# Two small constant tables of an attention kernel made from a memset and one index selection in place of two iotas

## The chip, the cores and the metric

The kernel runs on one core of one Trainium2 chip. The metric is the device time of one execution in microseconds. The kernel before took 751.49 us, the median of three runs that lie between 751.37 and 751.6. One execution was recorded by the hardware profiler; it took 750.43 us, and its first and last instruction are 748.9 us apart.

The engines are called as in the profile: PE (TensorE), PEld (its weight loads), DVE (VectorE), ACT (ScalarE), POOL (GpSimd) and SP (SyncE, which here only issues transfers). A name with a "q" (POOLq, SPq) is that engine's instruction queue. POOL's more complex instructions come in libraries of code that are loaded while the program runs; an instruction whose library is not known to be there has a load put ahead of it when the program is built, and the program can ask for a load by hand (`load_library`).

## The reference

Two blocks over 2048 tokens of width 640, with 32 heads of 20 columns, their outputs side by side:

```
# A: attention with a softmax
q, k, v = split_heads(A_x @ A_wqkv)
p = softmax(q @ k^T * 20**-0.5)
a = concat_heads(p @ v) @ A_wo

# B: linear attention
phi(t) = where(t > 0, t + 1, exp(t)) + 1e-6
num = phi(q) @ (phi(k)^T @ v);  den = phi(q) . sum(phi(k)) + 1e-6
b = concat_heads(num / den) @ B_wo

out = concat([a, b], axis=-1)          # (1, 2048, 1280), bf16
```

## The kernel before, in words

**The work.** Almost all of it lies in the class `_Fast`. Four heads make a group, each with 32 rows of the 128 partitions: 20 rows of data, one row (row 20 of the 32) that carries a constant, the rest zero. Scores are computed in blocks of 512 queries by 128 keys per head. A part of the exponentials is done by ACT (L1833, from PSUM to `f_PT`), another part by DVE and POOL with integer arithmetic (DVE L1731 writes `f_Sr`, POOL L1904 adds to it as 64-bit integers). PE then multiplies either with V. Projections, block B and the output projection are fitted between these steps.

**What sets the order.** A planner with estimated costs (`plan`, `run`) decides when the program is built in which order each engine gets its instructions, and `_Sched` adds the semaphore waits that the data needs. On the chip each engine takes its queue in that fixed order. The plan starts its clock at 8500 ns for all engines, behind the part that the change touches, and knows nothing of library loads.

**The start of the kernel.** `start_loads` (L1019) issues the first four tiles of x (tokens 0 to 511, 128 a tile, into `f_st`) from SP, the two weight strips for the first group of Q and K (`wst0`, part of the arena `f_ar`) from ACT's queue, then from SP the next 512 tokens, the weights of V, ten transposing loads for the last 1024 tokens (L1046), and the weights of K and Q (L1050, L1051).

`consts` (L1057), written out by hand, then does this:

- POOL makes an index table with an iota (L1060); DVE compares it with zero and so has the 128 x 128 identity `f_id` (L1065).
- POOL makes a second, two-column table of the partition numbers with another iota (L1067). That waits for DVE, because it overwrites the first. Then POOL is told to load library 1 by hand (L1069), the library of the 64-bit addition.
- DVE takes the partition number modulo 32 (L1070), and from it the masks: `kb` (1 or 16256 on row 20 of each 32, L1072 and L1074, and a bf16 copy, L1077) and `km` (1 or the factor `cq` on rows 0 to 19, L1078 and L1080).
- PE, meanwhile, runs 16 matmuls on zeros (`heat`, in the trace L156 with `f_zt`), waits for the identity, transposes the four tiles of x (20 transposes, L1093), and runs 8 more matmuls on zeros.
- DVE (L1100) and ACT (L1103) copy the transposed tiles to `f_xT`, two each.
- The two weight strips are spread into groups of 32 columns: DVE writes 20 columns of each (L1107), POOL the other 12 (L1110). Both parts of `wqp` are inputs of the first Q projection.
- POOL sets the column of ones in V and Vp (L1113, L1114).

Then POOL fills three Q buffers and seven groups of K with the constant rows out of the bf16 mask (`wprep`, L1124 and L1129) and clears two slices of the output weights (L1136).

The first steps of the plan are the Q projection of group 0 (PE, then DVE L1256 into `f_Qr`, with `km` and `kb` as factor and addend, and L1219 into `f_sq`), the K projection (L1256 into `f_KT`, L1235 into `f_ar`), tiles of V (L1303), and the first scores. The copies in `f_sq` and `f_ar` hold columns of other groups, which SP moves to their place with small transfers (L1195).

`_general` is a second, slower version of block A, taken only if a flag computed at the end asks for it. It has iotas of its own, and the change leaves it as it is.

Of the kernel before, what the change touches and what calls it, by code (L numbers as in the profile page):

```python
# [12 lines left out]
ALU = mybir.AluOpType  # L13
AX = mybir.AxisListType
# [3 lines left out]
D_HEAD = 20  # L18
# [751 lines left out]
class _Fast:  # L770
# [285 lines left out]

    def consts(self):  # L1057
        sch, ps = self.sch, self.ps
        it = self.it
        sch.op("pool", lambda e: e.iota(it[:, 0:128], [[1, 128]], base=0, channel_multiplier=-1),  # L1060
               writes=("it",))
        sch.op("dve", lambda e: e.memset(self.zt[:], 0.0), writes=("zt",))
        sch.op("dve", lambda e: e.memset(self.warm[:], 0.0), writes=("warm",))
        sch.op("act", lambda e: e.activation(self.warm[:], self.warm[:], AF.Exp), writes=("warm",))
        sch.op("dve", lambda e: e.tensor_scalar(self.ident[:], it[:, 0:128], 0.0, None, op0=ALU.is_equal),  # L1065
               reads=("it",), writes=("ident",))
        sch.op("pool", lambda e: e.iota(it[:, 0:2], [[0, 2]], base=0, channel_multiplier=1),  # L1067
               reads=("ident",), writes=("it",))
        self.nc.gpsimd.load_library(library_config.all_libraries[1])  # L1069
        sch.op("dve", lambda e: e.tensor_scalar(it[:, 2:4], it[:, 0:2], 31, None, op0=ALU.bitwise_and),  # L1070
               reads=("it",), writes=("it2",))
        sch.op("dve", lambda e: e.tensor_scalar(self.kb[:, 0:1], it[:, 2:3], float(D_HEAD), None, op0=ALU.is_equal),  # L1072
               reads=("it2",), writes=("kb0",))
        sch.op("dve", lambda e: e.tensor_scalar(self.kb[:, 1:2], it[:, 2:3], float(D_HEAD), 16256.0,  # L1074
                                                op0=ALU.is_equal, op1=ALU.mult),
               reads=("it2",), writes=("kb1",))
        sch.op("dve", lambda e: e.tensor_copy(self.kb16[:], self.kb[:]), reads=("kb0", "kb1"), writes=("kb16",))  # L1077
        sch.op("dve", lambda e: e.tensor_scalar(self.km[:, 1:2], it[:, 2:3], float(D_HEAD), None, op0=ALU.is_lt),  # L1078
               reads=("it2",), writes=("km1",))
        sch.op("dve", lambda e: e.tensor_scalar(self.km[:, 0:1], it[:, 2:3], float(D_HEAD), self.cq,  # L1080
                                                op0=ALU.is_lt, op1=ALU.mult),
               reads=("it2",), writes=("km0",))
        zt = self.zt

        def heat(k):
            for _ in range(k):
                sch.mm(ps[:, 6, 0:256], zt[:, 0:128], zt[:], start=True, stop=True, reads=("zt",),
                       writes=(("ps", 6),))
        heat(16)
        for t in range(4):  # L1090
            pb = ps[:, t, :].bitcast(BF16)
            for c in range(N_DC):
                sch.op("pe", lambda e, c=c, t=t, pb=pb: e.transpose(  # L1093
                    pb[:, 128 * c:128 * (c + 1)], self.stage[:, t, 128 * c:128 * (c + 1)], self.ident[:]),
                    reads=(("xn", t), "ident"), writes=(("ps", t),), inc=(c == N_DC - 1))
            heat(8 if t == 3 else 0)
            dst = self.xT[:, :, 128 * t:128 * (t + 1)]
            src = pb[:, 0:D_MODEL].rearrange("p (c m) -> p c m", c=N_DC)
            if t % 2 == 0:
                sch.op("dve", lambda e, dst=dst, src=src: e.tensor_copy(dst, src),  # L1100
                       reads=(("ps", t),), writes=(("xt", t),))
            else:
                sch.op("act", lambda e, dst=dst, src=src: e.copy(dst, src),  # L1103
                       reads=(("ps", t),), writes=(("xt", t),))
        for k, (wp, nm) in enumerate(((self.wqp, "wqp"), (self.wkp, "wkp"))):
            dst = wp[:, 0].rearrange("p c (i r) -> p c i r", r=32)
            sch.op("dve", lambda e, dst=dst, k=k: e.tensor_copy(  # L1107
                dst[:, :, :, 0:D_HEAD], self.wst0[:, k, :, 0:80].rearrange("p c (i d) -> p c i d", d=D_HEAD)),
                reads=(("wst0", k),), writes=((nm, 0),))
            sch.op("pool", lambda e, dst=dst, k=k: e.tensor_copy(  # L1110
                dst[:, :, :, D_HEAD:32], self.wst0[:, k, :, 80:128].rearrange("p c (i d) -> p c i d", d=12)),
                reads=(("wst0", k),), writes=((nm, 1),))
        sch.op("pool", lambda e: e.memset(self.V[:, :, :, 0:1], 1.0), writes=("Vones",))  # L1113
        sch.op("pool", lambda e: e.memset(self.Vp[:, :, :, 0:1], self.WP), writes=("Vones",))  # L1114
        sch.op("dve", lambda e: e.memset(ps[:, self.PVB, :], 0.0), writes=(("ps", self.PVB),))
        sch.op("dve", lambda e: e.memset(self.ones[:], 1.0), writes=("ones",))
        for e in self.free:
            self.free[e] = 8500.0
# [1206 lines left out]
```

## Time and profile before

| what | value |
|---|---|
| median of three runs | 751.49 us (751.37 to 751.6) |
| the profiled execution | 750.43 us |
| its span, first to last instruction | 748.9 us |
| PE busy | 721.3 us (96%) |
| ACT busy | 709.1 us (95%) |
| DVE busy | 619.9 us (83%) |
| POOL busy | 323.0 us (43%) |
| mean granted clock of PE | 0.989 |
| first POOL instruction of `consts` | starts at 9.19 us |
| first scores | start at 22.01 us |

A page of the profile gives the busy time of each engine, then the span in 40 equal slices (a digit is the busy share in tenths, and in the row PEclk the granted clock in tenths), and the chain that ended last, followed back from the last instruction to what released it at each step. The chain can also be printed in order of time, each piece with its start, its length and what it was. The timeline gives, for a group of equal instructions, its start, its length, engine, line, operation, output and input, shapes and count, and in brackets how long the engine had been idle before and which instruction ended that. In the table by stretches, each engine has its busy time and its instructions, followed by the granted clock, the busy share of the DMA engines and GB/s. "issue" is time in which the engine waited for nothing that the profile shows; a library load is not an instruction of the profile.

### The profile page before, as it was taken

The numbers are of one execution on the slowest core, as the hardware profiler recorded it, in microseconds if no ns is written. First come the engines' busy times: TensorE is split into PE (matmuls) and PEld (weight loads), VectorE is DVE, ScalarE is ACT, GpSimd is POOL, SyncE is SP. The second block draws the span as 40 slices with busy tenths as digits, with TensorE's granted clock in tenths as the row PEclk, the third lists the DMA queues.
The fourth block names the chain that finished last, engine by engine and source line by source line (L and its number), as shares of the span: only waits on it lengthen the run. The fifth ranks groups of instructions, "written<-read, shape, count | busy, mean of one in ns | idle before, by whom it ended". The sixth has DMA issues, their size and how long they took to land.

```text
span 748.9 us, 25688 instructions
## 1 busy us (share of the span) xinstructions
PE 721.3 (96%) x11193; PEld 254.7 (34%) x11193; DVE 619.9 (83%) x1179; ACT 709.1 (95%) x802; POOL 323.0 (43%) x313
## 2 busy tenths in 40 slices
PE   5999999999999999999999999999999999999995
PEld 3533333333222333333333333233233333332333
DVE  1888976787888888888889878899898989998973
ACT  1599999999999999999999999999999999999993
POOL 1924444054455444425433236642155554442550
PEclk7999999999999999999999999999999999999999
DMA  7411010101610100201101003011021100000001
GB/s 200 144 25 40 4 38 11 34 12 38 140 37 11 40 19 9 42 7 30 27 7 37 20 8 93 14 34 34 21 48 36 36 29 9 14 28 15 7 19 59
DMA packets 42611, 27.67 MB, mean 37 GB/s; under 512 B 26891, under 2 KB 41931, under 8 KB 42491
## 3 DMA queue, kind: packets, MB, share of 16 engines
q1 hardware_dynamic: 41178, 25.62, 13.2%
q8 instruction: 90, 1.47, 0.8%
q10 hardware_dynamic: 1312, 0.33, 0.2%
q14 instruction: 31, 0.25, 0.1%
HBM read 8.40 MB, written 5.24 MB: 18 GB/s over the span
## 4 chain that ended last, share of the span: by engine, by line
PE 44%; ACT 41%; DVE 6%; POOL 3%; issue 3%; DMA 1%; SPq 0%; DVEq 0%; POOLq 0%; ACTq 0%
PE ps L156 43%; ACT f_PT L1833 39%; POOL f_Sr L1904 3%; DVE f_Sr L1731 2%; ACT ps L1386 2%; DVE f_T L1924 1%; PE ps L1004 1%; DVE f_T L1931 1%; SPq L1195 0%; DVE f_ar L1388 0%; DMA f_ar<-in_B_x_dram 0%; DVE f_ar L1235 0%; DMA f_KT<-f_ar 0%; DVE f_ar L1384 0%; DVE f_sq L1219 0%
## 5 line engine op out<-in xcount | busy, mean ns | idle before, releaser
L1833 ACT ACTIVATE f_PT<-ps 128x1024 bf16<-128x1024 f32 x742 | 693.6, 1101 | 17.2 <-PE ps L156 16.0
L1904 POOL INT64_ADD f_Sr<-f_Sr x282 | 299.7, 1076 | 386.2 <-PE ps L156 293.0
L1731 DVE TENSOR_SCALAR f_Sr<-ps 128x512 int16<-128x512 f32 x564 | 381.0, 683 | 59.6 <-PE ps L156 53.7
L156 PE MATMUL ps<-f_Qr,f_KT 32*128 32x512 bf16 x2048 | 292.5, 384 | 5.6 <-ACT f_PT L1833 3.8
L156 PEld LDWEIGHTS ps<-f_Qr,f_KT 32*128 32x128 bf16 x2048 | 73.4, 91 | 247.3 <-ACT f_PT L1833 220.0
L156 PE MATMUL ps<-f_ar 128*32 128x320 bf16 (+4 forms) x3024 | 150.2, 295 | 1.1 <-DVE f_Sr L1731 0.4
L156 PE MATMUL ps<-f_PT,f_V 128*21 128x512 bf16 x1484 | 142.1, 382 | 0.0
L156 PE MATMUL ps<-f_Sr,f_V 128*21 128x512 bf16 x1128 | 103.6, 383 | 2.1 <-POOL f_Sr L1904 0.9
L156 PEld LDWEIGHTS ps<-f_ar 128*32 128x32 bf16 x3024 | 61.3, 95 | 63.9 <-issue 35.2
L156 PE MATMUL ps<-f_Sr,f_Vp 128*21 128x512 bf16 x564 | 54.1, 383 | 1.0 <-POOL f_Sr L1904 0.8
L156 PEld LDWEIGHTS ps<-f_PT,f_V 128*21 128x21 bf16 x1484 | 36.1, 90 | 42.8 <-issue 37.6
L156 PEld LDWEIGHTS ps<-f_Sr,f_V 128*21 128x21 bf16 x1128 | 26.5, 90 | 39.6 <-issue 19.1
L156 PE MATMUL ps<-f_ar,f_xT 128*32 128x160 bf16 x1280 | 37.1, 237 | 0.6 <-DVE f_ar L1235 0.4
L989 DVE CAST f_st<-ps 128x320 bf16<-128x320 f32 x60 | 28.6, 480 | 8.8 <-PE ps L156 8.6
L1388 DVE SCALAR_TENSOR_TENSOR f_ar<-ps,f_ar 128x320 bf16<-128x320 f32 (+1 forms) x52 | 28.9, 556 | 5.6 <-ACT ps L1386 5.0
L156 PE MATMUL ps<-f_xT,f_ar 128*32 128x512 bf16 x400 | 31.9, 396 | 0.3 <-DVE f_xT L1169 0.2
L156 PE MATMUL ps<-f_wo,f_OTd 128*32 128x320 bf16 (+1 forms) x608 | 31.6, 301 | 0.0
L1386 ACT ACTIVATE ps<-ps 128x320 f32<-128x320 f32 (+1 forms) x52 | 31.0, 596 | 0.0
L1384 DVE TENSOR_SCALAR f_ar<-ps 128x320 f32<-128x320 f32 (+1 forms) x52 | 28.8, 553 | 2.6 <-PE ps L156 2.6
L1924 DVE TENSOR_TENSOR f_T<-f_T,f_Rt 128x512 bf16<-128x512 f32 x32 | 29.4, 919 | 0.1
L156 PEld LDWEIGHTS ps<-f_ar,f_xT 128*32 128x32 bf16 x1280 | 23.6, 97 | 16.5 <-issue 9.6
L1303 DVE CAST f_V<-ps 128x160 bf16<-128x160 f32 x64 | 19.6, 316 | 10.4 <-PE ps L156 10.4
(72 smaller groups left out, 310.5 us busy)
## 6 DMA issues: line engine op xcount, KB each, us to landing
out_dram<-f_st SPq DMA_DIRECT2D x32, 160.0 KB
f_ar<-in_B_wqkv_dram SPq DMA_DIRECT2D x3, 800.0 KB
f_OTd<-f_OTn SPq DMA_DIRECT2D x105, 20.0 KB
f_Qr<-f_sq SPq DMA_DIRECT2D x88, 20.0 KB
f_KT<-f_ar SPq DMA_DIRECT2D x22, 80.0 KB
f_ar<-in_A_wqkv_dram SPq DMA_DIRECT2D x2, 800.0 KB
f_wq<-in_A_wqkv_dram SPq DMA_DIRECT2D x1, 800.0 KB
f_wo<-in_A_wo_dram SPq DMA_DIRECT2D x1, 800.0 KB
```

The costliest lines, as they stand in the source:

```text
L156: lambda e: e.matmul(out, lhsT, rhs, start=start, stop=stop, tile_position=tp, skip_group_check=sgc),
L989: (lambda e: e.tensor_copy(sl, ps[:, b, 0:320])), (("ps", b),), (("stage", s, h),),
L1004: self.sch.op("pe", lambda e, m=m: e.transpose(m["out"], m["in"], m["id"]), reads=m["reads"], writes=m["writes"], inc=m.get("inc", k == le ...
L1303: self.push("dve", lambda e: e.tensor_copy(dst, src), (("ps", b), "Vones"), (("V", t, r),), _c_dve(w), prio=1, after=None if isd else last)
L1384: self.push("dve", lambda e: e.tensor_scalar(r1, src, 0.0, 1e-6, op0=ALU.max, op1=ALU.add), (("ps", b),), (rk,), _c_dve(n), prio=1, ok=ok, ...
L1386: "act", lambda e: e.activation(src, src, AF.Exp), (), (("ps", b),), _c_act(n), prio=0,
L1388: "dve", lambda e: e.scalar_tensor_tensor(dst, src, 1.0, r1, op0=ALU.min, op1=ALU.add),
L1731: post = lambda: self.push("dve", lambda e: e.tensor_scalar(self.Sr[:, s, i, :], self.ps[:, b, :], 0.0, 32639.0 - self.PH[-1], op0=ALU.max ...
L1833: return _Op("act", lambda e: e.activation(self.PT[:, s0:s0 + n, :], ps[:, b0:b0 + n, :], AF.Exp, scale=math.log(2.0) / 128.0, bias=self.l ...
L1904: self.q["pool"].append(_Op("pool", lambda e: e.int64_add(v, v, inc), res, res, self.C64, self.C64 + 150, 0, self.seq, after))
L1924: "dve", lambda e: e.tensor_tensor(T2v, Tv, R.unsqueeze(2).broadcast_to([128, 16, 32]), op=ALU.mult),
L1931: self.push("dve", lambda e: e.transpose(self.T[:], ps[:, b, :]), (("ps", b),), ("T",), 630, prio=-1, after=freed, ok=lambda: n == 0 or (" ...
```

## The change

The change is in `consts` alone.

- Library 1 is asked for first, ahead of any POOL instruction of `consts`.
- The identity is made on POOL: a memset of `f_id` to 1, then one index selection (`affine_select`) that keeps the ones on the diagonal and writes zero elsewhere. Library 1 holds this selection as well. The comparison on DVE goes.
- The masks come from the identity. Row p has its one in column p, so among the columns 20, 52, 84 and 116 (column 20 of each block of 32) a row has a one exactly if p modulo 32 is 20, and among the columns 0 to 19 of each block exactly if p modulo 32 is below 20. Two maximum reductions on DVE (4 and 80 elements) give `kb[:, 0]` and `km[:, 1]`, and two products give the other two columns.
- Both iotas, the index table and the operation modulo 32 go.

```diff
     def consts(self):
         sch, ps = self.sch, self.ps
-        it = self.it
-        sch.op("pool", lambda e: e.iota(it[:, 0:128], [[1, 128]], base=0, channel_multiplier=-1),
-               writes=("it",))
+        self.nc.gpsimd.load_library(library_config.all_libraries[1])
+        idn = self.ident
+        sch.op("pool", lambda e: e.memset(idn[:], 1.0), writes=("ident",))
+        sch.op("pool", lambda e: e.affine_select(idn[:], idn[:], [[-1, 128]], ALU.is_equal, 0.0, base=0,
+                                                 channel_multiplier=1), writes=("ident",))
         sch.op("dve", lambda e: e.memset(self.zt[:], 0.0), writes=("zt",))
         sch.op("dve", lambda e: e.memset(self.warm[:], 0.0), writes=("warm",))
         sch.op("act", lambda e: e.activation(self.warm[:], self.warm[:], AF.Exp), writes=("warm",))
-        sch.op("dve", lambda e: e.tensor_scalar(self.ident[:], it[:, 0:128], 0.0, None, op0=ALU.is_equal),
-               reads=("it",), writes=("ident",))
-        sch.op("pool", lambda e: e.iota(it[:, 0:2], [[0, 2]], base=0, channel_multiplier=1),
-               reads=("ident",), writes=("it",))
-        self.nc.gpsimd.load_library(library_config.all_libraries[1])
-        sch.op("dve", lambda e: e.tensor_scalar(it[:, 2:4], it[:, 0:2], 31, None, op0=ALU.bitwise_and),
-               reads=("it",), writes=("it2",))
-        sch.op("dve", lambda e: e.tensor_scalar(self.kb[:, 0:1], it[:, 2:3], float(D_HEAD), None, op0=ALU.is_equal),
-               reads=("it2",), writes=("kb0",))
-        sch.op("dve", lambda e: e.tensor_scalar(self.kb[:, 1:2], it[:, 2:3], float(D_HEAD), 16256.0,
-                                                op0=ALU.is_equal, op1=ALU.mult),
-               reads=("it2",), writes=("kb1",))
+        iv = idn[:].rearrange("p (b c) -> p b c", c=32)
+        sch.op("dve", lambda e: e.tensor_reduce(self.kb[:, 0:1], iv[:, :, D_HEAD], axis=AX.X, op=ALU.max),
+               reads=("ident",), writes=("kb0",))
+        sch.op("dve", lambda e: e.tensor_reduce(self.km[:, 1:2], iv[:, :, 0:D_HEAD], axis=AX.XY, op=ALU.max),
+               reads=("ident",), writes=("km1",))
+        sch.op("dve", lambda e: e.tensor_scalar(self.kb[:, 1:2], self.kb[:, 0:1], 16256.0, None, op0=ALU.mult),
+               reads=("kb0",), writes=("kb1",))
         sch.op("dve", lambda e: e.tensor_copy(self.kb16[:], self.kb[:]), reads=("kb0", "kb1"), writes=("kb16",))
-        sch.op("dve", lambda e: e.tensor_scalar(self.km[:, 1:2], it[:, 2:3], float(D_HEAD), None, op0=ALU.is_lt),
-               reads=("it2",), writes=("km1",))
-        sch.op("dve", lambda e: e.tensor_scalar(self.km[:, 0:1], it[:, 2:3], float(D_HEAD), self.cq,
-                                                op0=ALU.is_lt, op1=ALU.mult),
-               reads=("it2",), writes=("km0",))
+        sch.op("dve", lambda e: e.tensor_scalar(self.km[:, 0:1], self.km[:, 1:2], self.cq, None, op0=ALU.mult),
+               reads=("km1",), writes=("km0",))
         zt = self.zt
```

## The prediction

> **What bounds the kernel now.** I read the page first: the span, the clock row and the chain that ended last.
>
> ```profile
> span 748.9 us, 25688 instructions
> ...
> PEclk7999999999999999999999999999999999999999
> ...
> PE 44%; ACT 41%; DVE 6%; POOL 3%; issue 3%; DMA 1%; SPq 0%; DVEq 0%; POOLq 0%; ACTq 0%
> ```
>
> TensorE (PE) and ScalarE (ACT) make 85% of the chain. The change touches neither. It touches the 3% called "issue", time in which an engine waited for nothing that the profile shows, and the first of the 40 slices is also the only one with a lower clock. So the second view was the chain of waits over the first 20 us (start, length, what).
>
> ```profile
> 0.92 0.01 POOLq L1060
> 0.93 8.26 issue
> 9.19 0.24 POOL f_ar L1060
> 9.45 0.24 DVE f_id L1065
> ...
> 10.11 0.01 POOLq L1069
> 10.12 5.99 issue
> ```
>
> POOL's queue handles something that belongs to L1060 (the first iota) and then does nothing for 8.26 us. It handles L1069, the call of load_library, and does nothing for 5.99 us. These are the two library loads: one that the iota asked for, one that the kernel asks for by hand. Behind the second stands a plain copy (next view, 16.11), which waits it out, so a load holds up whatever is behind it on POOL. The third view is the timeline around these two holes.
>
> ```profile
> 9.74 2.31 PE L1093 MATMUL ps<-f_id,f_st 128*128 128x128 bf16 x20 [5.02 <-DVE f_id L1065]
> 11.55 0.49 DVE L1100 COPY f_xT<-ps 128x640 bf16<-128x640 bf16 x1 [0.51 <-PE ps L1093]
> 11.84 1.91 PE L156 MATMUL ps<-f_zt 128*128 128x256 bf16 x8
> 12.09 0.69 ACT L1103 COPY f_xT<-ps 128x640 bf16<-128x640 bf16 x1 [0.38 <-PE ps L1093]
> 12.23 0.35 DVE L1107 COPY f_ar<-f_ar 128x400 bf16<-128x400 bf16 x1
> 16.11 0.37 POOL L1110 COPY f_wqp<-f_ar 128x240 bf16<-128x240 bf16 x1 [6.23 <-issue]
> 16.63 2.33 PE L156 MATMUL ps<-f_xT,f_wqp 128*32 128x512 bf16 x20 [2.87 <-POOL f_wqp L1110]
> 18.71 2.37 PE L156 MATMUL ps<-f_xT,f_ar 128*32 128x512 bf16 x20
> 19.00 0.81 DVE L1256 TENSOR_SCALAR f_Qr<-ps,f_km,f_kb 128x512 bf16<-128x512 f32 x1 [5.78 <-PE ps L156]
> 19.85 0.69 DVE L1219 TENSOR_SCALAR f_sq<-ps 128x512 bf16<-128x512 f32 x1
> 21.14 0.81 DVE L1256 TENSOR_SCALAR f_KT<-ps,f_km,f_kb 128x512 bf16<-128x512 f32 x1 [0.60 <-PE ps L156]
> 22.01 0.39 PE L156 MATMUL ps<-f_Qr,f_KT 32*128 32x512 bf16 x4
> ```
>
> The order is: identity, 20 transposes of x, 8 matmuls on zeros that keep PE warm (until 11.84 + 1.91 = 13.75), the first Q projection, the first K projection, the first scores at 22.01. The Q projection waits 2.87 us for POOL's copy of wqp, which stands behind the second load. Its other inputs were ready at 12.78 (12.09 + 0.69) and 12.58 (12.23 + 0.35). So the second load costs PE 16.63 - 13.75 = 2.88 us of idle time, and the first one sets when the transposes start.
>
> The fourth view is the table by stretches of 3.41 us (PE busy, PEld, DVE, ACT, POOL, granted clock, DMA share, GB/s).
>
> ```profile
> 4.83:8.24 3.41, 0.00 (x0) 0.00 (x0) 0.00 (x0) 0.00 (x0) 0.00 (x0) 1.00 1.10 373
> 8.24:11.65 3.41, 1.91 (x19) 1.92 (x20) 1.39 (x9) 0.63 (x1) 0.36 (x2) 0.50 1.22 279
> 11.65:15.06 3.41, 2.11 (x12) 1.25 (x10) 1.47 (x5) 0.75 (x2) 0.00 (x0) 0.50 0.51 113
> 15.06:18.47 3.41, 1.84 (x20) 0.90 (x24) 0.00 (x0) 0.00 (x0) 2.36 (x3) 0.50 0.40 91
> 18.47:21.88 3.41, 3.41 (x56) 1.78 (x45) 2.24 (x3) 0.00 (x0) 3.35 (x5) 0.50 0.81 197
> 21.88:25.29 3.41, 3.28 (x83) 1.98 (x76) 2.92 (x9) 2.85 (x4) 3.41 (x3) 1.00 0.89 316
> ```
>
> The clock falls to 0.50 after a stretch without PE work and comes back after the first stretch that is full. The idle gap splits the two stretches before that (2.11 and 1.84 of 3.41 us), so both projections ran at half clock.
>
> **The change, part by part.** *The second load goes.* POOL then meets the wqp copy right after the identity, far ahead of need, and 2.88 us of PE idle time vanish. What is late next is PE itself: the 8 matmuls on zeros end after the last inputs.
>
> *The first load becomes one of the other library.* Its length is not in the trace. The nearest rows are 8.26 us (same place, same DMA stream of 373 GB/s, other library) and 5.99 us (same library, with 113 GB/s around it in the fourth view). Nothing says which difference made it shorter, so I take the middle, 7.1, and keep both ends. The load then ends at 0.93 + 7.1 = 8.03.
>
> *The identity is made by a memset and a selection on POOL, in place of an iota there and a comparison on DVE.* Before, the first transpose started 9.74 - 9.19 = 0.55 us after the load. These rows bound the new pair and the new reductions:
>
> ```profile
> 33.77 1.17 POOL L1136 MEMSET f_wo<- 128x1280 bf16 x1
> 35.01 1.04 POOL L1904 INT64_ADD f_Sr<-f_Sr  x1
> 738.08 0.25 DVE L1999 TENSOR_REDUCE f_gm<-f_xT 128x1 f32<-128x96 f32 x1
> ```
>
> A memset of 128 columns is a tenth of the 1280, 0.12 us, taken as 0.2 with its start. The selection lies between the iota of as many elements (0.24) and the addition (1.04). I take 0.35, near the iota, which also steps through an index pattern. With 0.11 for two hand-overs (the 0.02 to 0.06 seen between rows) that makes 0.66: 0.1 later than before, between 0.1 earlier and 0.8 later.
>
> *DVE's masks.* Six small operations and the comparison become two reductions and three small operations. The reduction of 96 elements took 0.25, so 80 and 4 elements make at most 0.5, and three more about as much: some 0.9 us after the identity, while PE does the first five transposes. DVE then has 0.51 us idle ahead of its second copy of xT, so a delay of a tenth there is hidden. If that cover is gone, the same tenth goes on the path. The second iota's round trip (POOL to DVE and back) also goes. It lies under the transposes, so that is worth nothing.
>
> *The clock.* The first transpose comes at 8.03 + 0.66 = 8.69, 1.05 us earlier, and the warming matmuls end at 12.70. The Q projection starts at 12.72. PE is now busy without a gap from 8.69, so the stretch 11.65 to 15.06 is full and the clock should be back at 15.06 instead of 21.88. Q takes its 2.33 us to 15.05. K runs at full clock, for which there is a row:
>
> ```profile
> 27.41 1.26 PE L156 MATMUL ps<-f_xT,f_ar 128*32 128x512 bf16 x20 [0.23 <-DVE f_xT L1169]
> ```
>
> K ends by 16.4. DVE now sets the pace: Qr 2.37 us after Q's start (as 19.00 - 16.63), at 15.09. f_sq 0.85 later, at 15.94, and KT after its 0.69, at 16.63. The scores follow 0.87 later (22.01 - 21.14), at 17.50. So the scores come 22.01 - 17.50 = 4.5 us earlier.
>
> *The Trainium skill on the two disputed terms.* The row of the second load reads 5.99 us. The Trainium skill, GPSIMD Engine Reference, section "Instruction dispatch", gives about 6 us (5.95 measured) for freshly loaded code; the trace agrees for that load and not for the 8.26 of the first, and by its figure the sum would be the short-load rival below. The clock falls at 8.24 and rises at 21.88, 13.64 us apart, four times 3.41. The Trainium skill, TensorE: Matmul & The Clock Gate, section "The HAM clock gate", tells of a window of 3413 ns that runs freely and doesn't start with the kernel; the spacing agrees, and whether the windows lie at other places in other runs no run here shows. By that rule the rise would come anywhere from 12.1 to 15.5, and the sum would be 4.5 to 5.6.
>
> *Does it last to the end?* From 22 us on I followed the chain of waits. Its longest pieces are engine work:
>
> ```profile
> 104.35 56.95 PE ps L156 x997
> ...
> 185.53 76.24 ACT f_PT L1833 x83
> ```
>
> The order of instructions on each engine is fixed when the program is built, and the plan does not know the library loads, so everything behind the scores should move as one block. POOL gains even more: it copies without a pause from 16.11 until its first addition at 35.01, and all that would start about 7 us earlier. What does not move is SP's queue at the start:
>
> ```profile
> 2.88 15.07 SPq L1046 DMA_TRANSPOSE f_xT<-in_A_x_dram  x10
> ...
> 18.63 0.53 SPq L1051 DMA_DIRECT2D f_wq<-in_A_wqkv_dram  x1
> 20.57 8.66 SPq L1195 DMA_DIRECT2D f_Qr<-f_sq  x6
> ```
>
> SP issues transposing loads until 17.95 and two weight loads after them, and is free at about 19.2. Its spreads of f_sq can then start 1.4 us earlier, not 4.5. They fill Q buffers of later groups, so I take that as covered.
>
> The sum against the profiled execution's own time: 750.43 - 4.5 = 745.9. The median of the three runs is 751.49, 1.06 above it, so the forecast is 751.49 - 4.5 = **747.0 us**. A measurement here can tell about 0.2%, 1.5 us, from no change.
>
> **The rivals.** *A long load and no early clock (748.7).* The load takes the full 8.26, the transposes start at 9.85, Q at 13.88, and the clock isn't raised while Q and K run, because the stretch with transposes doesn't count as full. The whole shift is then 16.63 - 13.88 = 2.75. For it: the fourth view shows no stretch with transposes followed by a rise. Against it: none of those was full either. The Trainium skill's clock page, section "PE-mode transpose", says that transposes don't count as busy in the same way; no run so far shows it.
>
> *A short load (744.8).* At 5.99 the load ends at 6.92 and the transposes start at 7.58. Q follows at 11.61 and the clock is back at 11.65. Q ends at 12.9, Qr starts at 12.95, f_sq at 13.80, KT at 14.49, the scores at 15.36: 6.65 gained. For it: it is the same library. Against it: the DMA stream is then at its height. The inputs don't forbid it:
>
> ```profile
> 0.00:7.00 7.00, 3.59 (x16) 2.24 (x16) 0.17 (x2) 1.49 (x2) 0.20 (x4) 1.00 0.74 222
> ```
>
> 7 us at 222 GB/s are 1.55 MB, and the first four tiles of x and the two weight strips, issued first, make 0.98 MB by their shapes.
>
> *Held by SP (750.1).* If the spreads of f_sq do decide when a later group's scores start, only 1.4 us remain, within what can be told. For it: SP issues without a pause up to 19.2. Against it, the chain of waits from 20 to 80 us, by line, where SP has no share:
>
> ```profile
> by line: PE ps L156 78.4%; POOL f_Sr L1904 4.1%; ACT f_PT L1833 3.2%; DVE f_Sr L1731 3.1%; DVE f_KT L1256 2.5%; DVE f_ar L1235 2.0%; DVE f_xT L1169 2.0%; DVE f_V L1303 2.0%; DVE f_Qr L1256 1.4%; DVE f_sq L1219 1.2%; issue 0.7%
> ```
>
> *Two loads in a row (754.0, slower).* If the 8.26 us are paid by any first use of POOL's cores and not for the iota, the change doesn't do what it says: the early load comes on top. It ends at 0.93 + 8.26 + 5.99 = 15.18, the transposes start at 15.84, Q at 19.87. The clock is back at 21.88, Q ends at 22.04, and Qr, f_sq, KT and the scores follow at 22.1, 22.95, 23.64 and 24.5: 2.5 lost. It decides from a load of about 11 us on, where the warming matmuls would end at 16.6. For it: nothing shows which library is there at the start. Against it: the row ahead of the first hole names the iota's line.
>
> **How the numbers follow.** Forecast 0.49; long load without early clock 0.20; short load 0.17; held by SP 0.08; two loads 0.06. The first three are faster by over 0.2%: 0.86. The same: 0.08. Slower: 0.06. The range takes in the two loads' ends, 744.7 to 748.8, and leaves out 0.14.
>
> **What would show it.** Right: one hole on POOL, of 6 to 8.3 us, ending ahead of a memset and a selection; no load ahead of the wqp copy; the first Q projection within 0.1 us of the last matmul on zeros; clock 1.00 by about 15; first scores near 17.5; the piece of PE work that starts at 104.35 now near 99.9. Wrong: a second hole ahead of the copy, a selection over 1 us, clock 0.50 until 18 or later, or a shift at the scores that is no longer there at 104 or 185 us.

## The result and the profile after

| | before | changed kernel |
|---|---|---|
| median | 751.43 us (750.65 to 751.6, 4 runs) | 740.37 us (740.17 to 740.58, 4 runs) |
| profiled execution | 750.43 us | 740.17 us |
| its span | 748.9 us | 738.6 us |
| first scores | 22.01 us | 10.70 us |

The ratio is 0.9855, with a 95% interval of 0.9838 to 0.9872: 11 us faster, where 4.5 were forecast. The page of the changed kernel:

```profile
span 738.6 us, 25684 instructions
...
PEclk9999999999999999999999999999999999999998
...
PE 43%; ACT 42%; DVE 6%; POOL 6%; issue 1%; DMA 1%; SPq 0%; ACTq 0%; DVEq 0%; POOLq 0%
```

"issue" fell from 3% to 1% and POOL's share of the chain doubled. The timeline of the start shows why the first is so (start, length, engine, line, operation, output and input; in brackets the idle time ahead and what ended it):

```profile
0.96 0.20 POOL L1061 MEMSET f_id<- 128x128 bf16 x1 [0.45 <-POOLq L2304]
...
1.12 3.51 PE L156 MATMUL ps<-f_zt 128*128 128x256 bf16 x16 [1.12 <-DVE f_warm L1065]
...
1.24 0.29 POOL L1062 TENSOR_SCALAR_AFFINE_SELECT f_id<-f_id 128x128 bf16<-128x128 bf16 x1
1.57 0.16 DVE L1068 TENSOR_REDUCE f_kb<-f_id 128x1 f32<-128x4 bf16 x1 [0.49 <-POOL f_id L1062]
1.65 0.23 DVE L1070 TENSOR_REDUCE f_km<-f_id 128x1 f32<-128x80 bf16 x1
...
4.47 0.72 PE L1087 MATMUL ps<-f_id,f_st 128*128 128x128 bf16 x10
4.64 0.38 POOL L1104 COPY f_wqp<-f_ar 128x240 bf16<-128x240 bf16 x1 [3.10 <-DMA f_ar<-in_A_wqkv_dram]
...
5.49 0.73 PE L1087 MATMUL ps<-f_id,f_st 128*128 128x128 bf16 x10 [0.30 <-DMA f_st<-in_A_x_dram]
...
6.06 1.04 PE L156 MATMUL ps<-f_zt 128*128 128x256 bf16 x8
6.07 0.39 POOL L1104 COPY f_ar<-f_ar 128x240 bf16<-128x240 bf16 x1 [1.05 <-DMA f_ar<-in_A_wqkv_dram]
...
7.05 1.26 PE L156 MATMUL ps<-f_xT,f_wqp 128*32 128x512 bf16 x20
...
10.70 0.39 PE L156 MATMUL ps<-f_Qr,f_KT 32*128 32x512 bf16 x4
```

There is no hole at all. Library 1 is asked for (POOL's queue is done with the request at 0.93), and the memset starts at 0.96 us all the same. The identity is done at 1.53. Now the transposes start behind the 16 warming matmuls (1.12 to 4.63), and the second half of them waits 0.30 us for x itself. The 11.31 us at the first scores are made of four pieces: the transposes start 5.27 earlier (9.74 to 4.47); the transposes and the warming matmuls take 2.63 in place of 4.01 (1.38); the gap of 2.88 is gone; and from the Q projection to the scores it takes 3.65 in place of 5.38 (1.73). The last piece and most of the 1.38 are the clock, which no longer falls: Q takes 1.26 us in place of 2.33. (The rest, 0.05, comes from Q's start, which now lies that much ahead of the modelled end of the warming matmuls.)

Not all of it arrives. The same pieces of work, found in both chains of waits and timelines:

| what | before | after | earlier by |
|---|---|---|---|
| first scores on PE | 22.01 | 10.70 | 11.31 |
| PE's piece of 20.7 us, 317 matmuls | 37.75 | 27.18 | 10.57 |
| ACT's piece of 76.24 us, 83 exponentials | 185.53 | 174.85 | 10.68 |
| the flag at the end (DVE) | 741.39 | 730.41 | 10.98 |
| end of the span | 748.9 | 738.6 | 10.3 |

Two losses need a cause: 0.74 right behind the scores, and 0.7 behind the flag. The chain of waits of the changed kernel names the first:

```profile
1.32 4.70 DMA f_ar<-in_A_wqkv_dram
6.02 0.05 issue
6.07 0.39 POOL f_ar L1104
6.46 2.34 POOL f_V L1107
...
10.63 12.85 POOL f_KT L1123 x7
23.48 1.10 POOL f_wo L1130
24.59 1.03 POOL f_Sr L1898
25.62 0.04 issue
25.66 0.77 PE ps L156 x24
```

POOL's part of the start had been late because of the loads. Without them it begins when the second weight strip lands (6.02), and its fills (two Q buffers in the trace, seven groups of K and the output weights) still take until 24.59. PE, which moved further, waits there.

### The profile page after: what moved, and what is told of

It reads as the page before. It is cut to its first block, busy times and chain, and to the rows that moved or that the text cites. A ratio compares the mean times of both kernels' runs of the same rounds, so it can differ in the third digit from the quotient of the medians.

```text
span 738.6 us, 25684 instructions
## 1 busy us (share of the span) xinstructions
PE 716.7 (97%) x11193; PEld 252.7 (34%) x11193; DVE 619.6 (84%) x1177; ACT 709.2 (96%) x802; POOL 323.1 (44%) x313
## 4 chain that ended last, share of the span: by engine, by line
PE 43%; ACT 42%; DVE 6%; POOL 6%; issue 1%; DMA 1%; SPq 0%; ACTq 0%; DVEq 0%; POOLq 0%
PE ps L156 43%; ACT f_PT L1827 40%; POOL f_Sr L1898 3%; DVE f_Sr L1725 2%; ACT ps L1380 2%; POOL f_KT L1123 2%; DMA f_ar<-in_A_wqkv_dram 1%; DVE f_T L1918 1%; DVE f_ar L1382 1%; DVE f_T L1925 1%; PE ps L1004 1%; SPq L1189 0%; DMA f_KT<-f_ar 0%; POOL f_V L1107 0%; DVE f_ar L1378 0%
## 5 line engine op out<-in xcount | busy, mean ns | idle before, releaser
L156 PEld LDWEIGHTS ps<-f_Sr,f_V 128*21 128x21 bf16 x1128 | 26.5, 90 | 39.8 <-issue 19.3
```

The lines of the kernel that those rows point to most:

```text
L156: lambda e: e.matmul(out, lhsT, rhs, start=start, stop=stop, tile_position=tp, skip_group_check=sgc),
```

## The experiments

Two questions: why did the load of library 1 cost nothing, and what took back part of the gain? For the first, theory R says that a library stays loaded from one execution to the next. The kernel before ends with library 1 in place, so it pays for library 0 at its iota and again for library 1; the changed kernel finds what it left.

### The changed kernel, leaving the other library behind

```diff
             kf.run()
+            nc.gpsimd.load_library(library_config.all_libraries[0])
```

> The changed kernel, and after POOL's last addition the other library (number 0, the one with the iota) is asked for, so that the next execution does not find library 1 in place. Theory R (what an execution leaves loaded is still there for the next, and asking for a library that is there costs nothing): POOL's first memset now stands behind a hole of 6.0 to 8.3 us, first scores at 15.4 to 18.1, and the time is that of my sum for a real load, 744.8 to 747.6 us. Rival S (the load of library 1 is short whenever it comes at the very start, for its size or because no DMA runs yet): no hole, scores at 10.7, 740.4 us.

746.49 us (746.26 to 747.24), ratio 0.9941 (0.9925 to 0.9958). The chain of waits and, below it, POOL's timeline:

```profile
1.08 0.01 POOLq L1059
1.09 9.02 issue
10.11 0.20 POOL f_id L1061
10.31 0.07 issue
10.38 0.30 POOL f_id L1062
10.68 0.14 issue
10.82 2.29 PE ps L1087 x20
...
18.10 0.45 PE ps L156 x4
```

```profile
28.30 1.18 POOL L1130 MEMSET f_wo<- 128x1280 bf16 x1
31.11 1.04 POOL L1898 INT64_ADD f_Sr<-f_Sr  x1 [1.64 <-PE ps L156]
```

One line at the far end of the program brings the hole to its start, 9.02 us long, and a plain memset stands behind it. That is theory R; only the length lies outside the 6.0 to 8.3 us expected. It is also the kernel that I had forecast, with one real load: 4.8 us faster than the 751.26 beside it, scores at 18.10, and POOL's first addition waiting for PE and not the other way.

### The kernel before, leaving library 0 behind

The same line, added to the kernel before.

> The kernel before, with library 0 asked for after POOL's last addition. Theory R: the first hole (8.26 us) is gone, the iota runs at about 1 us, the second hole stays at 6.0 to 8.3 us under the stream, the wqp copy comes at 8 to 10.5 us, the scores at about 13 to 14.5, the time is 742.5 to 744 us. Rival S: the first hole belongs to library 0 and stays at 8.3 us, 751.4 us.

746.42 us (745.87 to 746.75), ratio 0.9938 (0.9921 to 0.9955).

```profile
1.15 0.24 POOL L1060 IOTA f_ar<- 128x128 int32 x1 [0.64 <-POOLq L2311]
1.72 0.13 POOL L1067 IOTA f_ar<- 128x2 int32 x1 [0.33 <-DVE f_id L1065]
10.93 0.37 POOL L1110 COPY f_wqp<-f_ar 128x240 bf16<-128x240 bf16 x1 [9.07 <-issue]
```

```profile
16.82 0.56 PE L156 MATMUL ps<-f_Qr,f_KT 32*128 32x512 bf16 x4
```

The first hole is gone, iotas and all, and the second is there. Rival S would have kept the first. The scores (16.82) and the time missed my 13 to 14.5 and 742.5 to 744, because the second load, now at the height of the DMA stream, took 9.07 us in place of 5.99, more than the 8.3 at most that I expected, and the clock fell meanwhile (to half from 10.37 to 17.20 in the trace's clock records; Q took 2.32 us).

### Both libraries at the start

```diff
+        self.nc.gpsimd.load_library(library_config.all_libraries[0])
         self.nc.gpsimd.load_library(library_config.all_libraries[1])
```

> The changed kernel with library 0 asked for right ahead of library 1, at the start. Theory R: library 1 is there, so both loads are real, 14 to 16.5 us together, first scores at 24 to 26.5, 753.5 to 756 us. Rival A (a load runs in the background and holds only an instruction that needs its code): memset at 1 us, hole only ahead of the selection. Rival S: one hole of 8.3 us for library 0, 747 to 748 us.

753.21 us (751.81 to 754.17), ratio 1.0031 (1.0019 to 1.0044).

```profile
0.93 8.09 issue
9.02 0.01 POOLq L1060
9.02 0.03 issue
9.05 0.01 POOLq L1060
9.06 5.71 issue
14.77 0.20 POOL f_id L1062
...
22.53 0.45 PE ps L156 x4
```

Both loads are real and stand in line: 13.8 us, and no instruction passes them. These loads did not run in the background (rival A). The loads together and the time came out just below what I expected (14 to 16.5 us, 753.5 to 756), the scores 1.5 us below (24 to 26.5): the clock was back at 18.33, and Q and K ran at full clock.

### The selection without the request for library 1

```diff
-        self.nc.gpsimd.load_library(library_config.all_libraries[1])
```

> The changed kernel without the line that asks for library 1 by hand, so that the identity by selection is left, but two libraries are asked for: number 0 ahead of the selection (the build takes the lowest number that holds it) and number 1 ahead of the first 64-bit addition. Theory R (a request costs time only if another library is in place): a hole of 8.0 to 9.1 us ahead of the selection, at the height of the DMA stream, and one of 5.7 to 6.0 us ahead of the first addition, which then comes at about 35; scores at 17.5 to 18.2. With the chain over POOL's first addition deciding, 750.5 to 751.5 us; if the scores decided, 747. Rival (the change pays because a selection is cheaper than two iotas and a round trip to DVE): close to 740.4.

755.27 us (754.61 to 756.1), ratio 1.0062 (1.0047 to 1.0078): slower than the kernel before, and outside what was expected.

```profile
0.80 0.20 POOL L1060 MEMSET f_id<- 128x128 bf16 x1 [0.29 <-POOLq L2303]
11.50 0.28 POOL L1061 TENSOR_SCALAR_AFFINE_SELECT f_id<-f_id 128x128 bf16<-128x128 bf16 x1 [10.49 <-issue]
...
29.40 1.16 POOL L1129 MEMSET f_wo<- 128x1280 bf16 x1
37.57 1.03 POOL L1897 INT64_ADD f_Sr<-f_Sr  x1 [7.01 <-issue]
```

The two holes are where theory R puts them, but counted from the request in POOL's queue they are 10.4 and 6.8 us long, and PE stands still from 33.74 to 38.65 for the addition behind the second (the chain has 3.82 us of "issue" right ahead of it). After that wait the clock is at half from 36.45 to 43.28 in the clock records, so that the flag at the end comes 4.3 us later than in the kernel before and the addition only 2.6. So without the line that names the library, the selection and the masks gain nothing. That line alone, ahead of the iotas, was not run.

### POOL's memsets of ones first

```diff
+        sch.op("pool", lambda e: e.memset(self.V[:, :, :, 0:1], 1.0), writes=("Vones",))
+        sch.op("pool", lambda e: e.memset(self.Vp[:, :, :, 0:1], self.WP), writes=("Vones",))
         for k, (wp, nm) in enumerate(((self.wqp, "wqp"), (self.wkp, "wkp"))):
...
-        sch.op("pool", lambda e: e.memset(self.V[:, :, :, 0:1], 1.0), writes=("Vones",))
-        sch.op("pool", lambda e: e.memset(self.Vp[:, :, :, 0:1], self.WP), writes=("Vones",))
```

> The changed kernel with POOL's two memsets of the columns of ones (2.39 and 0.81 us) put ahead of the copies of the weight strips, where POOL waits 3.10 us for a transfer. Theory P (behind the start, the chain runs over POOL's fills, first addition at 24.59 us, and this is why the end gained 10.3 us and the scores 11.3): first addition at about 22, 0.4 to 1.0 us faster, 739.4 to 740.0 us. Rival (the chain over POOL is only one of several that are late together): within 0.2 us of 740.4.

740.43 us (740.02 to 741.15). Run again, beside the changed kernel:

> The changed kernel with POOL's memsets of ones first, once more. Theory P, corrected by the first look at it (its clock rose only near 6.9 us, so PE itself was 0.75 us later than in the changed kernel and nothing was left to gain): with the clock's rise as early as in the changed kernel 0.4 to 0.7 us faster in single executions, on the mean 0 to 0.4 faster. Rival: no difference beyond 0.2.

> The changed kernel once more, beside the next one on the same chip: 740.2 to 740.6 us.

740.48 (740.02 to 741.26) against 741.08 (740.57 to 741.95, above the 740.2 to 740.6 expected): with over 1 us between the executions of one kernel, undecided. The first profile shows that the wait was turned round (POOL's timeline, then the chain of waits):

```profile
24.45 1.04 POOL L1898 INT64_ADD f_Sr<-f_Sr  x1 [2.71 <-PE ps L156]
```

```profile
11.45 0.45 PE ps L156 x4
...
27.18 1.05 PE ps L156 x10
```

POOL is 2.71 us early. From the first scores to the start of the piece of 317 matmuls (27.18 here as well) PE needs 15.73 us, as in the kernel before (15.74) and with one or two real loads (15.74 both), against 16.48 in the changed kernel. So the 0.74 behind the scores were POOL's. But PE had its first scores only at 11.45, since the clock rose only at 6.98 us (in the changed kernel at 4.42, both from the trace's clock records), and it lost another 0.38 at its next projection: 12 of its matmuls took 1.22 us from 27.83 on, against 0.83 in the changed kernel, with "issue" ahead of their weight loads. The second profile has the same stall (1.35 us); what it is stays open. Theory P holds for what is late next and is not shown to be worth a measurable time.

### The kernel before, kept warm

```diff
-            heat(8 if t == 3 else 0)
+            heat(24 if t == 3 else 0)
```

> The kernel before with 24 in place of 8 matmuls on zeros behind the transposes, which add no result: PE is kept busy in its 2.88 us gap, so the clock should be back before the Q projection at 16.6, Q and K run at full clock and the scores come at about 20.3 instead of 22.0. Theory C (the clock is a part of the gain by itself): 1.5 to 1.7 us faster, 749.8. Theory P (POOL's first addition at 35.0, for which PE already waits 0.23 us, comes no earlier): within 0.3 us of the kernel before.

748.87 us (748.28 to 749.58, 11 runs), ratio 0.9975 (0.9966 to 0.9984): 2.0 us faster, close to theory C's number. The profile contradicts that reading. Its chain of waits and, below it, the flag in the timeline:

```profile
35.19 1.04 POOL f_Sr L1904
36.22 0.04 issue
36.27 0.77 PE ps L156 x24
...
37.79 20.72 PE ps L156 x317
```

```profile
742.67 0.14 DVE L2013 TENSOR_SCALAR f_flag<-f_g 1x1 int32<-1x1 f32 x1
```

The scores did come at 20.48, 1.53 earlier. But POOL's first addition didn't, and the piece of 317 matmuls starts at 37.79, against 37.75 before. The clock's gain was lost there, as theory P said. (The clock records have its rise at 12.75, when four of the 24 matmuls had begun. So the place of the 3.41 us stretches brought it back in this execution, and the added matmuls at most held it.) Something else made it faster, and at the end of the span it can be seen: DVE wrote the flag at 742.67, 1.28 later than before (0.95 of it a wait of PE for a transfer into `f_OTd` at 240 us), and the span ended 5.0 us after it, against 7.5 us in the kernel before and 8.2 in the changed one.

### 16 small matmuls at the end

```diff
             kf.run()
+            for _ in range(16):
+                sch.mm(ps[:, 6, 0:32], kf.zt[:, 0:128], kf.zt[:, 0:32], start=True, stop=True, reads=("zt",),
+                       writes=(("ps", 6),))
```

In the trace's semaphore records (the views leave them out) PE's last instruction of the kernel before comes 2.46 us after that of every other engine, of the changed kernel 3.06, and in the kernel kept warm no later. The trace's packets show a block of 16 KB on an instruction queue just then, at 746.59 to 747.59 before and 735.79 to 737.25 after. In the kernel kept warm, PE's program is 32 instructions longer. The two waits differ by 0.60, which would be most of the 0.7 us that the changed kernel lost behind the flag.

> The changed kernel with 16 small matmuls on zeros (32 columns, no result used) at the end of PE's work, which make PE's program 32 instructions longer. Theory F (at the end PE waits 3.06 us longer than the other engines, because its last instructions lie in a block of code that is fetched only after the branch; 32 more instructions ahead move them to another block, as in the kernel with the longer warming): PE's last wait is gone, 737.3 to 738.2 us. Rival (that wait belongs to something at the end of the program that does not move with its length): 740.4 to 741.0.

> The kernel before with the same 16 small matmuls at the end. Theory F: 2.2 to 2.7 us faster than the kernel before, 748.4 to 749.0, with the clock, the loads and the first scores (22.0) as they were, so that the gain of the kernel with the longer warming is explained without its clock. Rival (that gain came from the clock): 751.

737.72 us (737.35 to 738.29), ratio 0.9825 (0.9812 to 0.9839), and 748.33 us (747.67 to 750.83, 11 runs), ratio 0.9976 (0.9966 to 0.9986). They are 2.65 and 2.41 us faster than without the useless work (the 740.37 of the changed kernel was not taken beside it, the 750.74 of the kernel before was). The flag of the changed kernel with them, from the timeline, and its page:

```profile
730.61 0.14 DVE L2007 TENSOR_SCALAR f_flag<-f_g 1x1 int32<-1x1 f32 x1
```

```profile
span 735.9 us, 25716 instructions
```

The flag is no earlier than in the changed kernel (730.41), and the span ends 5.3 us behind it in place of 8.2. PE's last wait is gone in both, as theory F forecast, and the rival's times are excluded. In the second kernel a block of 16 KB still comes at 746.11 to 747.50, but PE's last instruction had started at 746.08. That the wait is for the block that holds PE's last instructions is argued from these times and from what 32 instructions more do; no record names what a block holds, and no other length was run. The changed kernel with them is the fastest version that was run. (In the profiled execution of the second kernel the scores came at 20.94, against expectation: the clock had risen for a stretch from 14.04 to 17.45. At the flag, 741.10, 0.3 was left, about as much as POOL's first addition came earlier, 34.78 in place of 35.01.)

## Why the prediction was wrong, point by point

- **The second load: right.** The hole and PE's 2.88 us of idle time went as worked out.
- **The first load: the step that failed.** I wrote that it "becomes one of the other library" and bounded its length by the two holes in the trace, 5.99 and 8.26. That a request could cost nothing was not among the ends, although the trace ended with the very library that the changed kernel asks for first, and although my own rival of two loads says that nothing shows which library is there at the start. In place of 5.99 to 8.26 us the runs showed 0.03 us from the request to the memset. Of the 6.6 us between forecast (747.0) and result (740.37) this is nearly all: with a real load put back, the changed kernel takes 746.49, 4.8 less than the kernel before and not 11. So some 6 us of the gain hang on what the execution before left on POOL. That 746.49 is so near to the forecast is in part luck: the load was 1.9 us longer than the 7.1 of the sum, and the clock was back before Q and not behind it (from Q to the scores 3.62 us in place of 4.78).
- **Its length, where there is one: too short.** Holes that began in the first 2 us were 8.1 to 10.4 us long (8.26, 8.41, 8.33, 8.09 and 10.43 for library 0; 9.02 and 9.07 for library 1), with the DMA engines moving 276 to 311 GB/s meanwhile. Those that began after 9 us were 5.7 to 6.8 (5.99, 5.71, 6.06, 5.77, 6.77, all library 1), with 136 to 176 GB/s. So for library 1 the place was the difference, at the start the library made none that shows, and of my two rows the first was the nearer. That the stream is what makes the early ones long is likely but not shown: no load was run at the start without it. The Trainium skill's GPSIMD Engine Reference gives about 6 us ("Instruction dispatch"); the traces agree for the loads after 9 us and not for the early ones.
- **Identity and masks: right.** Selection 0.29 us (0.35 taken), reductions 0.16 and 0.23 (0.5 at most); behind a real load the first transpose came 0.71 us later (0.66 taken).
- **The clock: right in direction, rough in place.** The changed kernel never loses it, so the half-clock piece that I priced went altogether. A stretch need not be full either: in the profiled executions stretches with 2.68 us or more of PE's work out of 3.41 raised the clock, and those with 2.45 or less did not. The case in which transposes don't count is refuted here: with the load put back, PE's work from 10.82 on was transposes until 13.11, and the clock was back at 14.14, at the end of that stretch of 3.41. With both loads it was back at 18.33, and of the 2.86 us of work in that stretch at most 0.8 were not transposes; the stretch from 11.65 in the fourth view had 1.7 us of such work and didn't raise it. The Trainium skill, TensorE: Matmul & The Clock Gate, says otherwise for transposes ("PE-mode transpose"); the measurement decides.
- **"POOL gains even more": right with a real load, wrong without.** With the load put back POOL's fills ended 5.5 us earlier (29.48 in place of 34.94) and the scores came 3.9 earlier. Without a load POOL gained 10.44 us at its first addition (35.01 to 24.57) and PE 11.31 at the scores. I had not seen that PE already waited 0.23 us for this addition before.
- **Does it last: nearly.** As one block from 27 us to the flag, within 0.4, which is also what two executions of the changed kernel differ by at the flag (730.41 and 730.82). The end behind the flag was not in the forecast, and 0.7 us were lost there.
- **The rivals.** "Two loads in a row", built as a kernel of its own, came out at 753.2, against 754.0 worked out; that this is so near is in part luck, since its scores came at 22.53 and not at 24.5. Of the 11.31 us at the scores 10.98 are still there at the flag, so SP held at most 0.3.

## What to carry to other kernels

Before pricing a setup step (a library, a table, a buffer that must be loaded), ask what the execution before leaves in place: a program that ends in the state in which it starts may pay nothing, and a bound taken only from rows where the cost was paid has no end at zero. When a wait goes, follow the gain along several places of the trace, down to the end of the span, and not to the first that moves. And a number that comes out as forecast is no proof: the kernel kept warm gained what its clock should have given, for another reason.

## What was not expected of the hardware

- What POOL has loaded outlives an execution. All four combinations of first and last library behave so: where they were the same, POOL started at 0.96 and 1.15 us, and where not, behind a hole of 8.26 and 9.02 us. What a run of another program in between does was not tried.
- A load holds everything behind it on POOL, a memset or a copy too. It took 5.7 to 6.8 us where it began after 9 us (136 to 176 GB/s meanwhile) and 8.1 to 10.4 us in the first 2 us (276 to 311 GB/s).
- The clock's stretches of 3.41 us lay at another place in every profiled execution: the first recorded rise was between 3.80 and 6.98 us in ten of the profiled executions and at 12.75 and 15.97 in the other two. Ahead of the first record the tables show a clock of 1.00, but the 16 warming matmuls took 3.21 to 3.60 us, where 8 take 1.04 at full clock, so PE started at half.
- PE's last instruction came 2.46 us (before) and 3.06 us (changed kernel) after those of the other engines, with a block of 16 KB on an instruction queue just ahead of it. 32 more instructions of PE took this wait away in three kernels. That the wait is for the block that holds the last instructions is argued, not shown.
